# Fills on another engine, w1 kept in halves, masks in two ways and other orders of loads in an attention and expert kernel

## The chip, the cores and the metric

The kernel runs on one core of a Trainium2 chip. The time is device microseconds (us) of one execution; the kernel before took 395.87 us (median of 3 runs, 395.19 to 397.4). Five engines have queues of their own, each in order: TensorE (PE; its weight loads are listed as PEld), VectorE (DVE), ScalarE (ACT), GpSimd (POOL) and SyncE (SP, which only issues DMAs). Sixteen DMA engines move the data.

## The reference, cut to what matters

Attention over 4 batches, 8 heads, 768 positions and 64 numbers a head, and behind it a mixture of 4 experts that are all computed for every row:

```python
scores = q @ k.T / 8                       # causal
# heads 0, 2, 6 ("retrieval"): every earlier key
# heads 1, 3, 4, 5, 7 ("streaming"): keys 0..3 (sinks) and the last 64 keys
a = exp(scores - max); a = a / (a.sum() + 1e-9)
x = (a @ v) as rows of 8 * 64 = 512        # 3072 rows
p = domain_probs / (domain_probs.sum(-1) + 1e-9)
out = sum over e of p[:, e] * (relu(x @ w1[e]) @ w2[e])   # 512 -> 1024 -> 512
```

## The kernel before, in words

**Data.** w1 and w2 of all four experts are loaded once, cast to 16 bits by POOL's DMAs, and stay in SBUF (w1sb, w2sb). Rows are worked on in tiles of 128: four first tiles (the first 128 rows of each batch), then ten pairs of tiles. Attention goes in eight groups g = 2b + c (batch b, half c of 384 rows); the first tile of each batch is done by code of its own.

**The start (lines 381 to 482).** SP and ACT load q and k of the first tiles of batches 0 and 1 (load_first, L366), POOL everything else, in one written order: v of the first tiles, w1 of expert 0, q, k and v of the first tiles of batches 2 and 3, w2(0), w1(1), w2(1), w1(2), then k, q and v of group 0 (k_rows, q16, vR for the retrieval heads, vS for the windows of the streaming heads), w2(2) ahead of vS, the sinks (v_sinks, L285), w1(3), w2(3).

**Tiles 0 to 3 (L1497 to 1529).** For each: turn_first turns q and k on PE (L938), masks_first puts additive masks into PSUM by matmuls with the identity (L959), scores_first adds the scores to them (L971) and takes the exponential on ACT, values_first multiplies by v (L994), turn_back_first turns the result (L1015) into x_first. layer1_first (L1032) and plain_layer2 (L879) are expert 0.

**Experts 1 to 3 for the first tiles (moe_steps, L1465).** plain_steps: eight steps of layer 1 (L909, four matmuls of 512 columns each, Relu on ACT at L916), then layer 2 in two half steps for each of four tiles (L879, summed on DVE at L895). Between the steps small operations are put at numbered places: sums of weights (L795) for the Winograd form used later, prob_rows, and on ACT the fills (L1455): zeros in kS and kR, ones in vS, v_sinks and vR. A column of ones beside v makes the values matmul return the sum of the weights as well.

**The pairs (pair_steps, L1150).** Layer 1 plain (L1158) or in Winograd form (L1187), layer 2 in seven products of two halves (L1340). scale_inputs (L1109, DVE) scales xT, the attention's result, by the probabilities; before it, require(g) puts down whatever of group g is still missing.

**How attention is mixed in.** attention(b, c) (L489) is a generator that yields the estimated ns of each piece. The loop at the end (L1578) adds up the estimated time of the MoE steps and, by a plan of start and end for each group (L1545 to 1549), puts down attention steps until the group's own sum keeps pace. At a group's start it calls loads(a+1): k, q, and v of the retrieval heads of the next group (L209, L276). Within a group, in the order of heads 0, 2, 6, 1, 3, 5, 7, 4:

- turn_rows (group 0 only): k and q are turned on PE (L507). For all others SP does it by DMA transposes (transpose_rows, L229), put down in the group before: after the third head, or at the end of group 0.
- keys_to_rows (L244) and keys_to_windows in three parts (L262, L266, L270), DVE: copies of the turned keys for the retrieval and for the streaming heads.
- scores (L555, exponential L564, masks L571 and L575) and, some heads behind, values (L605 and L659).
- put_sinks (L295), a DMA that writes the sinks' rows into all windows of vS, issued by SP after the second head. The streaming heads' values (L659) read them.
- After a streaming head's values POOL loads the next group's window of v for that head (L278).
- The results go to xT: by SP transposes of x_one and x_pair (L641), and by DVE for the streaming heads (L679).

Of the kernel before, what the change touches and what calls it, by code (L numbers as in the profile page):

```python
# [19 lines left out]
def kernel(  # L20
# [34 lines left out]
    P = 128  # L55
# [46 lines left out]
    w1sb = pers.tile([P, E * DMP, F], FP16, name="w1sb")  # L102
# [27 lines left out]
    early = moe.tile([P, XS], FP16, name="early", tag="xs", bufs=1)  # L130
    warm = early[:, 1024:1536]
# [33 lines left out]
    def half(u):  # L165
        return slice(u * D, (u + 1) * D)
# [20 lines left out]
    def j0(c):  # L187
        return 0 if c else 1
# [40 lines left out]
    def transpose_rows(b, c):  # L229
        alloc_qT(b, c)  # L230
        for x, xr, at in ((kT, k_rows[b, c], P), (qTs[b, c], q16[b, c], 0)):
            for j in range(0 if at else j0(c), 3):
                nc.sync.dma_start(
                    out=x[:, :, at + j * P : at + (j + 1) * P],
                    in_=xr[:, j, :, :].rearrange("p h d -> p (h d)"),
                    transpose=True,
                )
# [54 lines left out]
    def put_sinks():  # L292
        x = windows(vSf).rearrange("p t s x -> p t (s x)")
        src = v_sinks.rearrange("p (t s) x -> p t (s x)", t=1)
        nc.sync.dma_start(out=x[0:NS, :, :], in_=src.to_broadcast([NS, WT, NSH * P]))  # L295

    def load_w1(e, f0, f1):
        x = moe_w1[e].rearrange("(u c d) f -> u d c f", u=2, c=DMP)
        for u in range(2):
            gp.dma_start(  # L300
                out=w1sb[half(u), e * DMP : (e + 1) * DMP, f0:f1],
                in_=x[u, :, :, f0:f1],
            )
# [5 lines left out]
    def w1_tile(e, ct, ft):  # L309

        return w_tile(e, w1sb[:, e * DMP + ct, :], ft)
# [54 lines left out]
    def load_first(eng, x, dst, b):  # L366
        x = x[b, :, 0:P, :].rearrange("(u h) (p j) d -> u p h (j d)", u=2, j=4)
        for u in range(2):
            eng.dma_start(out=dst[:, u, :], in_=x[u])
# [14 lines left out]
    for b in range(2):  # L384
        load_first(nc.sync, k, kf[b], b)
        load_first(nc.scalar, q, qf[b], b)
# [29 lines left out]
    fill(nc.vector, v_first[:, :, :, D : D + 2].rearrange("p b h x -> p (b h) x"), ONES)  # L416

# [3 lines left out]
    def warm_up(ps, n, cols):  # L421
# [5 lines left out]

    gp.memset(bias, 0.0)
    gp.affine_select(
        out=bias[:, 1, :], in_=bias[:, 1, :], compare_op=ALU.is_ge, fill=-60000.0,  # L430
        base=NW - 1, pattern=[[-1, P]], channel_multiplier=1,
    )
    gp.memset(bias[0:NS, 1, :], 0.0)
    gp.affine_select(
        out=bias, in_=bias, compare_op=ALU.is_ge, fill=-60000.0,
        base=0, pattern=[[0, 2], [1, P]], channel_multiplier=-1,
    )
# [18 lines left out]
    def load_first_all(b):  # L456
        for x, y, to in ((q, qf, qf_all), (k, kf, kf_all)):
            y[b] = to[:, b - 1, :, :].rearrange("p (u j) d -> p u (j d)", u=2)
            load_first(gp, x, y[b], b)
        load_first_v(b)  # L460

    load_first_v(1)
    load_w1(0, 0, F // 2)
    load_w1(0, F // 2, F)
    load_first_all(2)
    load_first_all(3)
    load_w2(0)
    load_w1(1, 0, F)
    load_w2(1)
    load_w1(2, 0, F)  # L470
# [7 lines left out]
    load_w1(3, 0, F)  # L478
# [10 lines left out]
    def attention(b, c):  # L489
# [218 lines left out]
        if g == 0:  # L708
            yield from turn_rows()
        keys_to_rows(b, c)  # L710
        yield 1500.0
        waiting = []
        for n, h in enumerate(order):
            v_steps, done = iter(()), None
            ahead = sum(len(score_tiles(x)) for x in (*waiting, h))
            if len(waiting) > 1 or (waiting and ahead > 6):
                done = waiting.pop(0)
                v_steps = values(done)
            for step in both(scores(h), v_steps):
                yield step  # L720
            if done is not None:
                behind_values(done)
            waiting.append(h)
            if n < 3:
                keys_to_windows(b, c, n)
                if c == 0:
                    yield 600.0
            if n == 1:
                put_sinks()
            if n == 2 and more and g:  # L730
                transpose_rows(*more)
# [3 lines left out]
        if g == 0:  # L735
            transpose_rows(*more)

    def small_things():
        def to_mask(x, bias):
            nc.vector.tensor_scalar(  # L740
                out=x, in0=bias, scalar1=0.0, scalar2=None, op0=ALU.is_ge
            )

        to_mask(mC, bias[:, 0, :])
        normalise(probs, psums, p_sb)

# [58 lines left out]
    def w1_part(e, j, k):  # L805
        c = e * DMP + j * KH
        return w1sb[:, c : c + KH, k * FN : (k + 1) * FN]
# [147 lines left out]
    def masks_first(b):  # L955
        ps_first[b] = [bank() for _ in range(2)]
        for u, ps in enumerate(ps_first[b]):
            for n in range(HG):
                nc.tensor.matmul(  # L959
                    out=ps[:, n * P : (n + 1) * P],  # L960
                    lhsT=ident16,
                    rhs=bias[:, 1 - RETR[u * HG + n], :].rearrange("m (p j) -> m j p", j=4),
                    start=(n == 0),
                    stop=False,
                    skip_group_check=True,
                )

    def scores_first(b):
        for n in range(HG):
            for u, ps in enumerate(ps_first[b]):  # L970
                nc.tensor.matmul(  # L971
                    out=ps[:, n * P : (n + 1) * P],
                    lhsT=qk_first[b][half(u), 1, n, :],
                    rhs=qk_first[b][half(u), 0, n, :],
                    start=False,
                    stop=True,
                    skip_group_check=True,
                )
        es_first[b] = []
        for ps in ps_first[b]:  # L980
            es = att.tile([P, 512], FP16, name="es", bufs=8)
            nc.scalar.activation(out=es, in_=ps, func=AF.Exp, scale=SC)
            es_first[b].append(es)
# [471 lines left out]
    def fills(i):  # L1455

        return [
            lambda: fill(nc.scalar, kSf[:, 0 : WT * NSH * P], 0.0),
            lambda: one_values(nc.scalar),
        ][2 * i :] + [  # L1460
            lambda: zero(nc.scalar, kR[i].rearrange("p c n t x -> p (c n) t x")),
            lambda: [one_values_r(nc.scalar, i, c) for c in range(NCH)],
        ]

    def moe_steps():  # L1465

        for e in range(1, E):
            sums = weight_sums(e - 1)
            sums.append(lambda e=e: last_weight_sum(e - 1))
            if e == E - 1:  # L1470
                more = first_weight_sums(EW[0])
                sums += more[:3]
            at = {}
            for n, op in enumerate(sums):
                at[n if e == E - 1 else 2 * n] = op
            if e == 1:
                at[FTP - 1] = prob_rows
                for n, op in enumerate(fills(0)):
                    at[FTP + 2 * n] = op
            if e == 2:  # L1480
                at[1] = lambda: load_probs(pair0)
                for n, op in enumerate(fills(1)):
                    at[FTP + 2 + 2 * n] = op
            if e == E - 1:
                at[FTP] = more[3]
                at[FTP + 1] = lambda: scale_inputs(pair0, 0)
                at[FTP + 3] = lambda: scale_inputs(pair0, EW[0])
                at[FTP + 5] = lambda: scaled_sums(EW[0])
            for n, step in enumerate(plain_steps(e)):
                yield step  # L1490
                if n in at:
                    at[n]()
        for n, nt0 in enumerate(pairs):
            yield from pair_steps(nt0, pairs[n + 1] if n + 1 < len(pairs) else None)


    nc.vector.memset(x_one[:, :, D:P], 0.0)  # L1497
    warm_up(ps_warm, 7, 512)
    masks_first(0)
    turn_first(0)  # L1500
    warm_up(pV.tile([P, 512], FP32, name="pV", bufs=2), 6, 128)
    scores_first(0)
    masks_first(1)
    values_first(0)
    turn_first(1)
    turn_back_first(0)
    scores_first(1)
    small_things()
    layer1_first(0, [0])
    values_first(1)  # L1510
    layer1_first(0, [1])
    turn_first(2)
    turn_back_first(1)
    masks_first(2)
    layer1_first(1, [0])
    scores_first(2)
    turn_first(3)
    masks_first(3)
    values_first(2)
    scores_first(3)  # L1520
    layer1_first(1, [1])
    turn_back_first(2)
    values_first(3)
    layer1_first(2)
# [22 lines left out]
    for a, n in zip(range(1, G), (0.75, 1.55, 2.55, 3.35, 4.35, 5.0, 6.65)):  # L1547
        plan[a] = (begin, first_pair + n * PAIR)
        begin = plan[a][1]
    state = {"a": 0, "steps": None, "done": 0.0}  # L1550

    def attention_step():

        a = state["a"]
        if state["steps"] is None:
            state["steps"] = attention(*divmod(a, NCH))
            state["done"] = 0.0
            if a < G - 1:
                loads(a + 1)
# [65 lines left out]
```

## Time and profile before

| | |
|---|---|
| median of 3 runs | 395.87 us (395.19 to 397.4) |
| profiled execution | 397.3 us, of which the trace spans 395.6 us |
| mean granted TensorE clock | 0.987 |
| busy: PE, PEld, DVE, ACT, POOL | 370.5, 310.4, 271.0, 227.6, 123.7 us |
| DMA | 40.41 MB, mean 102 GB/s; 62.8% of 16 engines' span in POOL's queue, 19.7% in that of SP and ACT |
| chain that ended last | PE 63%, DMA 12%, DVE 7%, POOL 7%, issue 5%, ACT 4% |
| first L1158 matmul (first pair of tiles) | at 93.67 us |

The busy rows tell how full an engine is over the whole span; the page's second part cuts the span into 40 slices of 9.89 us and shows the tenths of each slice that an engine was busy, the clock that the throttle granted PE, and the DMA engines' share. The list of waits says who waited for whom, with the sum, the number of times and the longest, all in us. In the time order of one engine each line has its start, its length, the line of code, the tile written and read, and in brackets the idle time before it with what ended it.

### The profile page before, as it was taken

What the parts mean: (1) busy time and instruction counts of PE and PEld (TensorE: products, weight loads), DVE (VectorE), ACT (ScalarE), POOL (GpSimd) and SP (SyncE); (2) the same over time, 40 slices, a digit from 0 to 9 for tenths busy, and PEclk for the clock granted to TensorE, in tenths of its full rate; (3) what the DMA queues carried; (4) which work ended last, traced back from release to release, by engine and by line L of the source; (5) the groups of instructions that cost most, each with busy time, mean ns of one, the idle gap of its engine ahead of it and who ended that gap; (6) DMA issues with size and microseconds to landing.
All of it is one profiled execution on the core that took longest, in us unless ns stands there. A gap on an engine that the chain in (4) does not pass through costs nothing.

```text
span 395.6 us, 10344 instructions
## 1 busy us (share of the span) xinstructions
PE 370.5 (94%) x4245; PEld 310.4 (78%) x4245; DVE 271.0 (68%) x599; ACT 227.6 (58%) x458; POOL 123.7 (31%) x160
## 2 busy tenths in 40 slices
PE   7799958998996899999999999899999999999997
PEld 4675423546985798899898899789899899998996
DVE  2544540789575768767967866966685976989882
ACT  2452517682865577778586696666477363351531
POOL 8672640746019308316637145610000000000000
PEclk9999996999999899999999999999999999999999
DMA  9999999999629969938999897991011030300101
GB/s 156 169 197 210 167 167 192 96 104 208 82 42 120 128 114 111 132 69 108 130 135 137 92 154 54 131 155 56 15 65 55 2 109 0 106 5 1 56 3 53
DMA packets 132744, 40.41 MB, mean 102 GB/s; under 512 B 119880, under 2 KB 125608, under 8 KB 132696
## 3 DMA queue, kind: packets, MB, share of 16 engines
q0 software_dynamic: 98400, 20.34, 62.8%
q1 hardware_dynamic: 33144, 17.84, 19.7%
q10 hardware_dynamic: 1152, 1.57, 1.3%
q8 instruction: 33, 0.54, 0.6%
q14 instruction: 15, 0.12, 0.1%
HBM read 47.00 MB, written 6.34 MB: 135 GB/s over the span
## 4 chain that ended last, share of the span: by engine, by line
PE 63%; DMA 12%; DVE 7%; POOL 7%; issue 5%; ACT 4%; SPq 0%; POOLq 0%; ACTq 0%; DVEq 0%
PE pO L1340 23%; PE pA L1158 18%; PE pO L1187 8%; DMA w1sb<-in_moe_w_dram 8%; PE pA L555 4%; DMA vS<-in_v_dram 2%; PE pA L909 2%; PE pV L1187 2%; POOL vS L278 2%; PE pA L1187 2%; PE pO L879 2%; PE pV L605 1%; DMA xT<-x_pair 1%; ACT rc L674 1%; PE pV L659 1%
## 5 line engine op out<-in xcount | busy, mean ns | idle before, releaser
L1340 PEld LDWEIGHTS <-hA 128*128 128x128 f16 x1104 | 104.9, 98 | 12.2
L1158 PE MATMUL pA<-xs,w1sb 128*128 128x256 f16 x768 | 98.0, 275 | 0.0
L1158 PEld LDWEIGHTS <-w1sb 128*128 128x128 f16 x768 | 72.5, 99 | 8.0
L1340 PE MATMUL pO<-w2sb,hA 128*128 128x256 f16 x640 | 78.0, 272 | 0.0
L1167 ACT ACTIVATE hA<-pA 128x512 f16<-128x512 f32 x96 | 56.5, 597 | 34.5 <-PE pA L1158 24.9
L564 ACT ACTIVATE es<-pA 128x384 f16<-128x384 f32 (+2 forms) x112 | 52.3, 493 | 28.4 <-PE pA L555 28.1
L278 POOL DMA_DIRECT2D vS<-in_v_dram x40 | 37.3, 936 | 97.7 <-PE pV L659 93.0
L1340 PE MATMUL pO<-tsb,hA 128*128 128x256 f16 x464 | 57.2, 273 | 0.0
L1109 DVE TENSOR_TENSOR xs<-xT,pB 128x512 f16<-128x512 f16 (+1 forms) x53 | 47.2, 914 | 4.4 <-DMA xT<-x_pair 3.0
L795 DVE TENSOR_TENSOR hA<-hA 128x1024 f16<-128x1024 f16 x60 | 39.5, 684 | 0.4
L1187 PEld LDWEIGHTS <-w1sb 128*128 128x128 f16 x512 | 31.3, 98 | 1.2 <-issue 0.4
L909 PE MATMUL pA<-x_first,w1sb 128*128 128x512 f16 x96 | 24.5, 408 | 6.7 <-ACT hA L916 6.7
L879 PE MATMUL pO<-w2sb,hA 128*128 128x512 f16 x128 | 29.7, 379 | 1.2 <-DVE acc L895 1.2
L679 DVE TENSOR_TENSOR xT<-pV,rc 64x256 f16<-64x256 f32 (+1 forms) x40 | 19.4, 488 | 11.3 <-ACT rc L683 10.5
L555 PE MATMUL pA<-qT,kR 128*128 128x128 f16 (+2 forms) x132 | 22.8, 266 | 3.4 <-DVE kR L244 3.4
L1360 ACT COPY s<-pO 128x256 f32<-128x256 f32 x31 | 11.5, 372 | 25.0 <-PE pO L1340 19.0
L209 POOL DMA_DIRECT2D k_rows<-in_k_dram x24 | 21.3, 896 | 14.2 <-PE pA L507 10.9
L1204 DVE CUSTOM_DVE_ANT_0 hA<-pO,s 128x512 f16<-128x512 f32 x26 | 17.7, 688 | 10.3 <-PE pO L1187 8.5
L1197 ACT COPY s<-pO 128x512 f32<-128x512 f32 x39 | 22.7, 588 | 3.2 <-PE pO L1187 2.9
L674 ACT ACTIVATE rc<-pV,eps 64x256 f32<-64x256 f32 (+1 forms) x40 | 20.9, 522 | 5.6 <-PE pV L659 4.5
L909 PEld LDWEIGHTS <-w1sb 128*128 128x128 f16 x96 | 9.5, 103 | 18.4 <-issue 9.8
L879 PEld LDWEIGHTS <-hA 128*128 128x128 f16 x128 | 12.2, 98 | 14.3 <-issue 1.7
(161 smaller groups left out, 542.0 us busy)
## 6 DMA issues: line engine op xcount, KB each, us to landing
pB<-p_rows SPq DMA_DIRECT2D x10, 512.0 KB, 4.1
out_dram<-o SPq DMA_DIRECT2D x19, 256.0 KB, 2.0
w2sb<-in_moe_w_dram POOLq DMA_DIRECT2D x4, 1024.0 KB, 12.3
w1sb<-in_moe_w_dram POOLq DMA_DIRECT2D x6, 512.0 KB, 11.9
k_rows<-in_k_dram POOLq DMA_DIRECT2D x24, 128.0 KB, 4.8
q<-in_q_dram POOLq DMA_DIRECT2D x20, 128.0 KB, 4.9
vS<-in_v_dram POOLq DMA_DIRECT2D x20, 112.0 KB, 4.5
vS<-in_v_dram POOLq DMA_DIRECT2D x20, 80.0 KB, 4.1
```

What stands on the lines that cost most here:

```text
L278: gp.dma_start(out=t[:, t0(c) :, own_v(h)], in_=windows_of(v, b, h, c))
L555: nc.tensor.matmul(out=ps[:, o : o + nq], lhsT=key_tile(b, c, h, t), rhs=qTs[b, c][:, hp, q0 : q0 + nq], start=True, stop=True,)
L564: nc.scalar.activation(out=es[:, 0:cols], in_=ps[:, 0:cols], func=AF.Exp, scale=SC)
L674: nc.scalar.activation(out=rc[r, lo:], in_=ps[o, lo:CH], func=AF.Ln, bias=eps[o, :])
L795: nc.vector.tensor_tensor(out=out, in0=a, in1=b, op=ALU.subtract)
L879: nc.tensor.matmul(out=ps_o, lhsT=hs[:, ft, nt * P : (nt + 1) * P], rhs=w2sb[:, e * FTP + ft, :], start=(ft == 0), stop=(ft == FTP - 1),)
L909: nc.tensor.matmul(out=ps, lhsT=w1_tile(e, ct, ft), rhs=x_first[:, ct, :], start=(ct == 0), stop=(ct == DMP - 1),)
L1109: nc.vector.tensor_tensor(out=o, in0=xin, in1=pb.to_broadcast([P, DMP, n, P]), op=ALU.mult)
L1158: nc.tensor.matmul(out=ps[:, f * PC : (f + 1) * PC], lhsT=w1_tile(e, ct, f0 + f), rhs=xs[:, ct, :], start=(ct == 0), stop=(ct == DMP - 1),)
L1167: nc.scalar.activation(out=blocks[:, b0 : b0 + 2, k0 : k0 + 2, :].rearrange("p t f x -> p f t x"), in_=ps.rearrange("p (f t x) -> p f t x" ...
L1187: nc.tensor.matmul(out=ps[:, f * P : (f + 1) * P], lhsT=w_tile(e, w[:, ct, :], f), rhs=a[:, ct, :], start=(first and f == 0 and ct == 0), ...
L1340: nc.tensor.matmul(out=ps, lhsT=a[:, k, :], rhs=b(k), start=(first and k == 0), stop=(k == KT - 1), skip_group_check=not first,)
```

## The change

1. The ones in vS, v_sinks and vR are filled by DVE at the very start instead of by ACT in experts 1 and 2. ACT keeps the zeros.
2. w1sb is laid out by expert and half of the 1024 columns, and loaded half by half: four DMAs an expert instead of two (expert 0 had four before).
3. Tiles 0 and 1 get their additive masks ahead of everything else on PE, with the bias laid out so that the matmuls read it in order; tiles 2 and 3 have no mask matmuls, but a multiplication by 0 and 1 on DVE after the exponential. Six short warm-up matmuls go. The order of the first tiles' steps is another one.
4. q and k of batches 0 and 1 are spread differently over SP and ACT; w1's halves lie between the first rows of batches 2 and 3.
5. The next group's loads are put down two groups ahead (loads(g+2) after the sixth head); group 1's, after turn_rows of group 0.
6. The transposes of q for the next group come at a group's start, those of k after its first head; in group 0 both after the fourth head.
7. keys_to_windows: part 0 at the start, parts 1 and 2 after the first head, with one 600 ns step instead of three.
8. put_sinks is issued by POOL, at a group's start, instead of by SP after the second head.
9. Sums of weights, scale_inputs and the plan's ends are moved.

```diff
-    w1sb = pers.tile([P, E * DMP, F], FP16, name="w1sb")
+    w1sb = pers.tile([P, E * 2, DMP, F // 2], FP16, name="w1sb")
...
-        nc.sync.dma_start(out=x[0:NS, :, :], in_=src.to_broadcast([NS, WT, NSH * P]))
+        gp.dma_start(out=x[0:NS, :, :], in_=src.to_broadcast([NS, WT, NSH * P]))
...
-    for b in range(2):
-        load_first(nc.sync, k, kf[b], b)
-        load_first(nc.scalar, q, qf[b], b)
+    for eng, x, y, b, u in (
+        (nc.scalar, q, qf, 0, 0), (nc.scalar, q, qf, 0, 1), (nc.scalar, k, kf, 0, 1),
+        (nc.sync, k, kf, 0, 0), (nc.sync, k, kf, 1, 0), (nc.sync, k, kf, 1, 1),
+        (nc.scalar, q, qf, 1, 0), (nc.sync, q, qf, 1, 1),
+    ):
+        load_first(eng, x, y[b], b, u)
...
+    one_values(nc.vector)
+    for i in range(2):
+        for c in range(NCH):
+            one_values_r(nc.vector, i, c)
...
     load_first_v(1)
-    load_w1(0, 0, F // 2)
-    load_w1(0, F // 2, F)
-    load_first_all(2)
-    load_first_all(3)
+    load_w1(0, 0)
+    load_first_rows(2)
+    load_w1(0, 1)
+    load_first_rows(3)
+    load_first_v(2)
+    load_first_v(3)
     load_w2(0)
...
         if g == 0:
             yield from turn_rows()
+            loads(1)
+        elif more:
+            transpose_q(*more)
+        put_sinks()
         keys_to_rows(b, c)
+        keys_to_windows(b, c, 0)
         yield 1500.0
...
-            if n < 3:
-                keys_to_windows(b, c, n)
+            if n == 0:
+                keys_to_windows(b, c, 1)
+                keys_to_windows(b, c, 2)
+                if more and g:
+                    transpose_k(*more)
                 if c == 0:
                     yield 600.0
-            if n == 1:
-                put_sinks()
-            if n == 2 and more and g:
-                transpose_rows(*more)
+            if n == 3 and not g:
+                transpose_k(*more)
+                transpose_q(*more)
+            if n == 5 and g + 2 < G:
+                loads(g + 2)
         for h in waiting:
             yield from values(h)
             behind_values(h)
-        if g == 0:
-            transpose_rows(*more)
...
+    def masks_behind():
...
+            nc.vector.tensor_scalar(
+                out=out, in0=src.to_broadcast(list(out.shape)), scalar1=0.0,
+                scalar2=None, op0=ALU.is_ge,
+            )
...
             nc.scalar.activation(out=es, in_=ps, func=AF.Exp, scale=SC)
+            if not masked:
+                nc.vector.tensor_tensor(
+                    out=es, in0=es,
+                    in1=mask_first[:, u, :, :].rearrange("p h x -> p (h x)"),
+                    op=ALU.mult,
+                )
...
+            lambda: zero(nc.scalar, kR[i].rearrange("p c n t x -> p (c n) t x")),
             lambda: fill(nc.scalar, kSf[:, 0 : WT * NSH * P], 0.0),
...
+        put(E - 1, 5, lambda: scale_inputs(pair0, 0))
+        put(E - 1, FTP, more[3])
+        put(E - 1, FTP + 2, lambda: scale_inputs(pair0, EW[0]))
+        put(E - 1, FTP + 4, lambda: scaled_sums(EW[0]))
...
+    masks_behind()
     warm_up(ps_warm, 7, 512)
     masks_first(0)
+    masks_first(1)
     turn_first(0)
-    warm_up(pV.tile([P, 512], FP32, name="pV", bufs=2), 6, 128)
     scores_first(0)
-    masks_first(1)
+    turn_first(1)
     values_first(0)
-    turn_first(1)
-    turn_back_first(0)
     scores_first(1)
...
-    for a, n in zip(range(1, G), (0.75, 1.55, 2.55, 3.35, 4.35, 5.0, 6.65)):
+    for a, n in zip(range(1, G), (0.7, 1.55, 2.55, 3.4, 4.4, 5.3, 6.65)):
...
-            if a < G - 1:
-                loads(a + 1)
```

## The prediction

> **What bounds the kernel now.** I read the page's busy shares and slices first, then the waits, then the chain and the stretches where PE idles.
>
> ```profile
> PE 370.5 (94%) x4245; PEld 310.4 (78%) x4245; DVE 271.0 (68%) x599; ACT 227.6 (58%) x458; POOL 123.7 (31%) x160
> ...
> PE   7799958998996899999999999899999999999997
> ...
> PEclk9999996999999899999999999999999999999999
> DMA  9999999999629969938999897991011030300101
> ```
>
> PE works in 370.5 of 395.6 us, so only its 25 us of idle time and its slow stretches can be won. The dips in PE's row are slice 5, slice 12 and a shallow one near slice 25; the first two come with a lower clock. The DMA row is full for the first ten slices: until about 99 us nothing lands earlier just because it is asked for earlier. The waits and the two-microsecond stretches (PE, PEld, DVE, ACT, POOL busy, clock, DMA share, GB/s) name hole 1:
>
> ```profile
> ACT vS L343 <- DMA vS<-in_v_dram: 11.1, 1, 11.1
> ```
> ```profile
> 54.00:56.00 2.00, 0.49 (x3) 0.10 (x1) 0.48 (x1) 0.00 (x0) 0.59 (x2) 1.00 2.27 149
> 56.00:58.00 2.00, 0.00 (x0) 0.00 (x0) 0.00 (x0) 0.08 (x1) 2.00 (x3) 1.00 0.72 47
> 58.00:60.00 2.00, 0.00 (x0) 0.00 (x0) 0.00 (x0) 2.00 (x5) 0.13 (x1) 0.79 0.95 170
> 60.00:62.00 2.00, 0.76 (x2) 0.26 (x2) 0.00 (x0) 2.00 (x6) 0.00 (x0) 0.50 1.09 195
> 62.00:64.00 2.00, 2.00 (x6) 0.76 (x5) 0.00 (x0) 1.22 (x3) 0.00 (x0) 0.50 1.10 186
> ```
>
> ACT's fill of ones in vS waits 11.07 us for the window loads of v, which land at 57.8; the Relus behind it wait too; PE runs out of banks and idles 6.75 us (54.49 to 61.24). Then the granted clock is 0.50 until about 66, so 4.8 us of matmuls do 2.4 us of work. Hole 1 is 9.2 us. Hole 2, in time order on DVE:
>
> ```profile
> 124.70 0.56 DVE L679 TENSOR_TENSOR xT<-pV,rc 64x384 f16<-64x384 f32 x1
> 128.28 1.22 DVE L1109 TENSOR_TENSOR xs<-xT,pB 128x1024 f16<-128x1024 f16 x1 [3.01 <-DMA xT<-x_pair]
> 129.42 0.83 DVE L244 COPY kR<-kT 64x768 f16<-64x768 f16 x2
> ```
>
> x_pair was ready at 117.34, but SP issued its transpose at 122.75, after five transposes of k and q (3.83 + 3.62 us). PE idles 3.37 us (126.45 to 129.82), then runs at half clock from 131 to 134: 3.4 + 1.7 = 5.1 us. Hole 3 (251 to 258.6, attention group 6, clock 1.00) is 2.7 us: v rows landing late, then values waiting for DVE.
>
> **Which transfers wait on POOL.** One pattern decides my forecast:
>
> ```profile
> 27.29 0.88 POOL L209 DMA_DIRECT2D k_rows<-in_k_dram  x1 [1.19 <-DMA w2sb<-in_moe_w_dram]
> ...
> 37.69 0.76 POOL L276 DMA_DIRECT2D vR<-in_v_dram  x1 [4.50 <-DMA w2sb<-in_moe_w_dram]
> ...
> 55.41 0.54 POOL L285 DMA_DIRECT2D v_sinks<-in_v_dram  x1 [4.67 <-DMA w2sb<-in_moe_w_dram]
> ```
>
> Counting POOL's DMAs in order, these are the 25th, 28th and 39th, and each waits for the one eight before it (17th, 20th, 31st, all w2): POOL has eight in flight. They also land in order: the first vS load, issued at 45.25 behind w2 of expert 2, lands 10.4 us later.
>
> **The change part by part.** All sums are against the profiled execution, 397.3 us (span 395.6 plus 1.7 around it); the median of the runs shown is 395.87, 1.4 lower.
>
> *Ones on DVE.* ACT loses 1.21 + 0.41 + 0.30 + 0.31 us of copies and the wait. DVE gains two fills of 448 and 672 words; from its 256-word fill (L402, 0.27 us) 0.5 and 0.7, with the small ones 1.6 us. They lie in DVE's idle 2.66 to 8.41, while PE waits for q and k, as do the three mask fills (0.9 us by L740's 0.18 for 128 columns, after POOL's bias at 4.0). Nothing on the path; if that cover went, 2.5 us.
>
> *Masks.* Sixteen L959 matmuls of tiles 2 and 3 go: 2 x 1.09 us on a dense PE. Four DVE multiplies come, 0.45 us each by L571's 0.36 for 384 columns, with layer-1 matmuls emitted in between. The other masks move into the wait for q (5.93).
>
> *First loads.* The second half of k of batch 0 becomes ACT's third DMA instead of SP's second: 0 to +1 us at 7.28; I take +0.6, one issue.
>
> *w1 in halves.* The wait at 14.28 (1.40 us) goes. POOL issues 16 instead of 10 w1 DMAs, 6 x 0.64 = 3.8 us, hidden in its waits of 4.50 and 4.67; the bytes are the same. w2 of expert 0 still lands at 27.05, and its layer 2, now at 28.37, can start 1.3 us earlier at most. So expert 1 starts 1.5 us earlier (0 to 3).
>
> *Hole 1's place.* Without it PE would reach the streaming heads' values of group 0 far earlier. Following the loop at the end of the file by hand: two of the three 600 ns steps go, so more of group 0 is put down per MoE step, and head 1's values move from expert 3's second tile to the end of expert 2. Expert 2 starts at 50.87 - 1.5; then 7.07 + 7.07 us of L909 and L879, 1.2 of turns and 4.9 of scores and values as their rows last: head 1's values are reached at about 70.5, latencies included.
>
> They read vS with the sinks in it. put_sinks leaves SP (59.47 before) for POOL, behind the nine DMAs of loads(1). By the count of eight, loads(1)'s second vR waits for w2 of expert 3, and put_sinks, the 58th, for the second k load. w2 of expert 3 lands at 70.4 (57.19 + 13.2). The same kinds of loads of group 0 moved 784 KB from 42.6 to 47.6, so the 912 KB of loads(1) take 5.8 us and the sinks land at 70.4 + 5.8 + 0.3 = **76.5**. PE idles 6 us there. This wait takes hole 1's place. Bounds: 73 (as soon as POOL can issue) to 80.
>
> The Trainium skill, DMA: Bandwidth & Descriptors, section "Queues, rings and completion order", says that a DMA engine alternates between queue rows packet by packet and consumes one row's ring in order; so the same 35 KB from SP's row would not stand behind k, q and vR. The trace's 10.4 us of the vS load agrees for POOL's row. By that rule the sinks left on SP would land near 60, and the sum would be that of rival A below.
>
> After 76.5 PE has seven score and value blocks (2.0 us), expert 3's 32 + 32 matmuls (6.9 + 6.9) and the half clock (2.2, between holes 1 and 2): the first pair starts at 76.5 + 18.0 = 94.5, against 93.67. **+0.8.** The move of weight sums and of scale_inputs to step 5 adds no instruction; x_pair, now behind six transposes of 1.25 us on SP, lands near 81, before DVE asks (about 85): hidden.
>
> *Holes 2 and 3.* Loads two groups ahead, q turned at a group's start and k after its first head leave SP free when x_pair is ready: -5.1 (bounds -2 to -5.1: DVE is busy 6.6 of the 9 us from 126, and the window copies now come together). Hole 3: rows of v are long there, and group 6 is spread from 5.3 pairs on: -2.7 (0 to -2.7). Of PE's small waits at 116 to 123 (1.55 us) half: -0.8.
>
> *put_sinks in later groups.* Its chain from a group's first streaming values: vS and sinks issues 0.9 + 1.8, loads 7.7, four vS 3.6, landing 4.5, put_sinks 3.2: 21.5 us. By the new order the next group's first streaming values come 20 us later in group 2 and 18.7 in group 4, by a count of dense matmuls that ignores DVE. 0 to 4.3 us; I take +1.5, a third, since DVE (above 0.9 busy around 186 to 198) paces PE there.
>
> **Sum.** +0.8 - 5.1 - 2.7 - 0.8 + 1.5 = -6.3 us: 391.0 for the profiled execution, 389.6 at the median; I say 389.5.
>
> **Rivals.**
> - *A: the sinks land in time*, before PE asks. For it: hole 1's cause does vanish. Against: the count of eight. Then x_pair behind q's transposes (q lands 75.5; x_pair 81) holds DVE at scale_inputs; PE has banks for two tiles of layer 2 and starts the pair near 88.5: -5.2 - 7.1, **383.5**.
> - *B: nothing takes hole 1's place*: -9.2 - 1.5 - 7.1, **378**. It needs k, q and v of group 1 some 8 us earlier, and the DMA row is full.
> - *C: holes 2 and 3 fill again* because DVE, not SP, bounds those stretches (252 to 262: DVE 0.9 and more): only 2 of 8.6 us come, **396**.
> - *D, slower: put_sinks on POOL is late in groups 2 and 4.* If DMA contention adds 4 us to its landing (the vS loads at 45 took 10 instead of 4.5), the stalls are 5.5 and 6.8 us, each with 2 us of half clock: 16.3 instead of 1.5, **404**. It decides from where these stalls exceed 1.5 + 6.3 = 7.8 us together.
> - That the fills don't do what they say has no room: nothing writes vS before the fills on DVE.
>
> **Chances.** Forecast 0.52, A 0.17, B 0.07, C 0.12, D 0.12. The forecast's own range is 386 to 393. With A and C in and B and D out (0.19), 382 to 397. A measurement of this kernel tells 0.5% (2 us) from no change: faster is the forecast, A and B and a little of C, 0.78; same most of C, 0.10; slower D, 0.12.
>
> **What would show it.** No ACT wait at the fill of ones. PE idle at head 1's values of group 0, waiting for vS, and clock 0.50 after it (A and B: none, or DVE waiting for x_pair instead). First L1158 near 94.5. x_pair's transposes issued within 2 us of their x_pair, PE dense where hole 2 was. The forecast is wrong if the sinks of group 0 land well before or after 76.5, or if PE waits for vS in groups 2 and 4.

## The result and the profile after

The changed kernel takes 407.34 us (median of 4 runs, 404.0 to 409.3) against 395.53 (4 runs, 394.99 to 397.4): a ratio of 1.028, 95% interval 1.020 to 1.036. The forecast was 389.5, with 397 as the upper end: wrong in sign. Ratios here leave out executions that were disturbed, so that a ratio need not be the quotient of the medians beside it.

The profiled execution took 404.0 us (span 402.3, mean clock 0.975), 6.7 more than the one of before. It is the shortest of its four, and the one of before the longest of its; the other 5 us of the medians' difference lie in executions without a trace. From the page, busy rows and slices (10.06 us each):

```profile
PE 368.9 (92%) x4223; PEld 309.2 (77%) x4223; DVE 273.0 (68%) x614; ACT 224.8 (56%) x450; POOL 132.3 (33%) x175
...
PE   7779997099997989999499999999999999999997
...
PEclk9999999579998999999989999999999999999999
```

PE's row has no dip in slice 5 any more (hole 1 is gone, and no wait of ACT for vS is left), but slice 7 is empty, slices 7 and 8 have a clock of 0.5 and 0.7, and slice 19 is a new dip. The waits, and in time order of PE the four lines that hold most of its idle time behind 69 us:

```profile
PE pV L678 <- DMA vS<-v_sinks: 17.5, 3, 11.6
```
```profile
80.78 0.39 PE L678 MATMUL pV<-es,vS 128*128 128x32 f16 x5 [11.55 <-DMA vS<-v_sinks]
...
125.05 0.34 PE L678 MATMUL pV<-es,vS 128*128 128x48 f16 x7 [2.27 <-DVE xT L698]
...
142.07 0.29 PE L678 MATMUL pV<-es,vS 128*128 128x32 f16 x5 [1.37 <-DMA vS<-v_sinks]
...
201.80 0.37 PE L678 MATMUL pV<-es,vS 128*128 128x32 f16 x5 [4.61 <-DMA vS<-v_sinks]
```

Three times PE stands at a group's first streaming values and waits for the sinks in vS: 11.55 us in group 0, 1.37 in group 2, 4.61 in group 4. The clock falls with them: in stretches (columns PE, PEld, DVE, ACT, POOL, clock, DMA share, GB/s) it is already 0.50 while PE still waits:

```profile
70.00:72.00 2.00, 0.00 (x0) 0.00 (x0) 1.04 (x3) 0.00 (x0) 0.66 (x1) 0.87 2.35 157
74.00:76.00 2.00, 0.00 (x0) 0.00 (x0) 0.00 (x0) 0.00 (x0) 0.38 (x1) 0.50 2.39 155
78.00:80.00 2.00, 0.00 (x0) 0.00 (x0) 0.00 (x0) 0.00 (x0) 0.00 (x0) 0.50 1.68 113
```

What POOL issued in that time:

```profile
71.34 0.77 POOL L283 DMA_DIRECT2D vR<-in_v_dram  x1 [4.63 <-DMA w2sb<-in_moe_w_dram]
72.30 0.77 POOL L283 DMA_DIRECT2D vR<-in_v_dram  x1 [0.18 <-issue]
73.70 0.68 POOL L302 DMA_DIRECT2D vS<-v_sinks  x1 [0.63 <-issue]
```

put_sinks is the last of ten DMAs of group 0's start. The second vR load waits for w2 of expert 3, as the count of eight had it; the sinks are issued at 73.70 and land 7.0 us later. The first pair of tiles starts at 97.63 instead of 93.67 (+4.0), and from there to the end the kernel takes 304.7 us instead of 301.9 (+2.7).

### The profile page after: what moved, and what is told of

Its sections match the earlier page's. It is cut to its first block, busy times and chain, and to the rows that moved or that the text cites. A ratio compares the mean times of both kernels' runs of the same rounds, so it can differ in the third digit from the quotient of the medians.

```text
span 402.3 us, 10304 instructions
## 1 busy us (share of the span) xinstructions
PE 368.9 (92%) x4223; PEld 309.2 (77%) x4223; DVE 273.0 (68%) x614; ACT 224.8 (56%) x450; POOL 132.3 (33%) x175
## 4 chain that ended last, share of the span: by engine, by line
PE 45%; DVE 3%; DMA 1%; ACT 1%; issue 0%; DVEq 0%
PE pO L1389 18%; PE pA L1207 12%; PE pO L1236 7%; PE pA L574 2%; PE pV L1236 2%; PE pA L1236 1%; DMA vS<-v_sinks 1%; PE pV L678 1%; DVE hA L836 1%; PE pV L624 1%; DVE xs L1158 1%; DVE xT L698 1%; PE pA L1481 0%; ACT hA L1216 0%; DVE o L1412 0%
## 5 line engine op out<-in xcount | busy, mean ns | idle before, releaser
L1389 PEld LDWEIGHTS <-hA 128*128 128x128 f16 x1104 | 106.5, 99 | 14.0 <-DVE hA L836 0.6
L1207 PE MATMUL pA<-xs,w1sb 128*128 128x256 f16 x768 | 97.0, 273 | 0.0
L1207 PEld LDWEIGHTS <-w1sb 128*128 128x128 f16 x768 | 71.7, 98 | 7.4
L583 ACT ACTIVATE es<-pA 128x384 f16<-128x384 f32 (+2 forms) x112 | 51.4, 495 | 26.6 <-PE pA L574 23.8
L594 DVE TENSOR_TENSOR es<-es,mW 128x256 f16<-128x256 f16 (+1 forms) x40 | 12.7, 321 | 32.5 <-ACT es L583 32.4
L1236 PEld LDWEIGHTS <-w1sb 128*128 128x128 f16 x512 | 31.2, 98 | 1.5 <-issue 0.7
L678 PE MATMUL pV<-es,vS 128*128 128x56 f16 (+2 forms) x240 | 13.1, 189 | 20.2 <-DMA vS<-v_sinks 17.5
L698 DVE TENSOR_TENSOR xT<-pV,rc 64x256 f16<-64x256 f32 (+1 forms) x40 | 19.5, 489 | 14.7 <-ACT rc L702 14.0
L678 PEld LDWEIGHTS <-vS 128*128 128x128 f16 x240 | 11.4, 98 | 22.2 <-DMA vS<-v_sinks 12.0
L949 PE MATMUL pA<-x_first,w1sb 128*128 128x512 f16 x96 | 23.5, 400 | 0.0
L919 PEld LDWEIGHTS <-hA 128*128 128x128 f16 x128 | 12.1, 98 | 13.4 <-ACT hA L956 0.3
```

The lines of the kernel that those rows point to most:

```text
L583: nc.scalar.activation(out=es[:, 0:cols], in_=ps[:, 0:cols], func=AF.Exp, scale=SC)
L678: nc.tensor.matmul(out=ps[:, q0 : q0 + nq], lhsT=v_tiles(b, c, h)[:, t, :], rhs=es[:, o : o + nq], start=(n == 0), stop=(n == len(work) - ...
L698: nc.vector.tensor_tensor(out=xT[g][r, ct, lo:], in0=ps[r, lo:CH], in1=rc[r, lo:], op=ALU.mult)
L919: nc.tensor.matmul(out=ps_o, lhsT=hs[:, ft, nt * P : (nt + 1) * P], rhs=w2sb[:, e * FTP + ft, :], start=(ft == 0), stop=(ft == FTP - 1),)
L949: nc.tensor.matmul(out=ps, lhsT=w1_tile(e, ct, ft), rhs=x_first[:, ct, :], start=(ct == 0), stop=(ct == DMP - 1),)
L1207: nc.tensor.matmul(out=ps[:, f * PC : (f + 1) * PC], lhsT=w1_tile(e, ct, f0 + f), rhs=xs[:, ct, :], start=(ct == 0), stop=(ct == DMP - 1),)
```

## The experiments

The theory, T1: put_sinks in POOL's queue, behind loads(1), costs the time. The rivals: other parts of the change cost it (T2), or the place in POOL's queue has no effect and only the late issue counts (T1b). Each kernel ran beside the kernel before on the same chip.

**1. The ones alone.** Before, with the fills of ones moved to VectorE's start:

```diff
+    one_values(nc.vector)
+    for i in range(2):
+        for c in range(NCH):
+            one_values_r(nc.vector, i, c)
...
-            lambda: one_values(nc.scalar),
...
-            lambda: [one_values_r(nc.scalar, i, c) for c in range(NCH)],
```

> The kernel before with one part of the change: the fills of ones in vS, v_sinks and vR are done by VectorE at the start; the zeros stay with ScalarE, put_sinks with SyncE. T1 (the loss of the changed kernel comes from put_sinks standing behind POOL's loads): with the sinks left on SP, nothing takes hole 1's place but the loads themselves: ScalarE's 11.1 us wait for vS goes, PE is dense at 54 to 61, the first pair of tiles starts near 85 to 88 instead of 93.67, total 387 to 390 (6 to 9 us less than before's 395.5). T2 (hole 1 is only the face of a limit by the transfers, which would show at the next place, w1 and w2 of expert 3 landing near 63 and 70): the first pair starts at 91 to 94, total 393 to 396.

386.99 us (385.95 to 388.01) against 396.31; ratio 0.978 (0.973 to 0.982). The first pair starts at 85.66, 8.0 earlier. Its page:

```profile
PE   8799999989987999999999999799999999999996
...
PEclk9899999999999999999999999999999999999999
```

Hole 1 is gone and the clock holds from slice 2 on. This part of the change gives the upper end of T1's 6 to 9 us, as long as SP puts the sinks.

**2 and 3. put_sinks on POOL alone, and with the ones.** In both one line is changed, at the old place behind the second head; the second of the two has the ones of experiment 1 as well:

```diff
-        nc.sync.dma_start(out=x[0:NS, :, :], in_=src.to_broadcast([NS, WT, NSH * P]))
+        gp.dma_start(out=x[0:NS, :, :], in_=src.to_broadcast([NS, WT, NSH * P]))
```

> The kernel before with one part of the change: put_sinks is issued by POOL at its old place, after the second head. T1: in group 0 it stands behind loads(1) in POOL's queue and lands near 80, and the streaming heads' values of group 0 are asked for near 79 there (ScalarE's wait for vS has already delayed everything by 9 us), so only 0 to 2 us are lost there; in later groups the sinks land some 3 us later than from SP: total 396 to 399. T2 (put_sinks on POOL costs nothing, the other parts of the change do): 395 to 396. If the queue hurts in groups 2 and 4 by itself: 400 or more, with PE waits for vS of 4 us and more there.

403.45 us (398.78 to 405.41); ratio 1.015 (1.008 to 1.022). More than T1's 396 to 399. In the profiled execution, the longest of the four, hole 1 is still there (PE idles 8.81 us, 6.75 before), and PE waits 1.75 us for the sinks in group 0, 1.11 in group 4 and 4.07 in group 6.

> The kernel before with both: ones by VectorE at the start and put_sinks issued by POOL at its old place, after the second head. T1: the gain of the first is eaten by the second: PE reaches the streaming heads' values of group 0 near 70 and waits until the sinks land near 78 to 81, half clock after it; the first pair of tiles starts at 94 to 98, total 396 to 402, and the difference to the kernel with the ones alone is 8 us or more. T2 (put_sinks on POOL costs nothing): as the kernel with the ones alone, within 2 us.

407.13 us (404.92 to 408.38); ratio 1.028 (1.023 to 1.032): the changed kernel's time, from two of its nine parts. Against experiment 1 one line costs 20.1 us. In time order on PE and POOL:

```profile
80.02 0.39 PE L663 MATMUL pV<-es,vS 128*128 128x32 f16 x5 [9.67 <-DMA vS<-v_sinks]
...
259.35 0.37 PE L663 MATMUL pV<-es,vS 128*128 128x32 f16 x5 [4.32 <-DMA vS<-v_sinks]
```
```profile
70.98 0.78 POOL L276 DMA_DIRECT2D vR<-in_v_dram  x1 [4.22 <-DMA w2sb<-in_moe_w_dram]
...
73.35 0.68 POOL L295 DMA_DIRECT2D vS<-v_sinks  x1 [0.64 <-DVE tsb L799]
```

The same wait at the same place as in the changed kernel; the first pair starts at 96.23, 10.6 us behind experiment 1. The other 9 us come behind that, in later groups: PE idles 3.9 us more there and loses 5.4 us to the clock, which experiment 1 does not lose. Half of that follows the 4.32 us wait in group 6, the other half hole 2, where PE waits 4.07 us for kR instead of 2.31. T2 is out for group 0.

**4. The changed kernel with put_sinks on SP, at its new place.**

```diff
-        gp.dma_start(out=x[0:NS, :, :], in_=src.to_broadcast([NS, WT, NSH * P]))
+        nc.sync.dma_start(out=x[0:NS, :, :], in_=src.to_broadcast([NS, WT, NSH * P]))
```

> The changed kernel with one part undone: put_sinks is issued by SyncE again, at the new place (a group's start). T1: PE's 11.6 us wait for vS in group 0 goes, as the sinks land near 60 to 62; the first pair of tiles starts at 88 to 91 instead of 97.6 (x_pair behind six transposes on SP may then hold VectorE); the waits in groups 2 and 4 get shorter by the 3 us that the landing took in POOL's queue: total 394 to 397 against 407.3. T2 (the masks, the window copies, the order of loads cost the time): first pair 96 or later, total 404 to 407.

395.06 us (10 runs, 392.2 to 399.66); ratio 0.996 (0.992 to 0.999). The sinks are issued at 57.41, no engine waits for them in group 0, and the first pair starts at 87.84: 9.8 us earlier than in the changed kernel. In the medians this line is worth 12.3 us, all of the change's loss, as T1 said. On SP and PE:

```profile
57.41 0.82 SPq L302 DMA_DIRECT2D vS<-v_sinks  x1
```
```profile
69.52 0.29 PE L678 MATMUL pV<-es,vS 128*128 128x32 f16 x5 [0.15 <-DVE es L594]
```

But three waits stay:

```profile
84.32 3.68 PE L919 MATMUL pO<-w2sb,hA 128*128 128x512 f16 x16 [2.51 <-DVE acc L935]
...
131.56 0.29 PE L678 MATMUL pV<-es,vS 128*128 128x32 f16 x5 [1.49 <-DMA vS<-v_sinks]
...
190.50 0.37 PE L678 MATMUL pV<-es,vS 128*128 128x32 f16 x5 [3.82 <-DMA vS<-v_sinks]
```

The first is rival A's: VectorE waits 2.67 us for x_pair, whose transpose stands on SP behind six others. The other two show that the engine of put_sinks is not what makes it late in groups 2 and 4 of this order of work.

**5. put_sinks on POOL, but ahead of loads(1).**

```diff
         if g == 0:
             yield from turn_rows()
+            put_sinks()
             loads(1)
```

> The changed kernel with one step moved: in group 0 put_sinks goes ahead of loads(1), still in POOL's queue. In later groups nothing changes. T1a (POOL's DMAs land in the order in which they were issued): the sinks are issued near 59, but land behind w1 and w2 of expert 3, near 70.5 to 71.5; PE, which asks at 69, waits 1.5 to 2.5 us instead of 11.6, with little half clock: total 393 to 396 against 407.3. T1b (what cost the time is only the late issue, behind the nine loads; landing takes 3 to 4 us from any queue): the sinks land near 63, PE doesn't wait for them at all in group 0: the same total less 2 to 4 us. T2 (PE's wait has another cause than the place in POOL's queue): 404 or more. The waits in groups 2 and 4 (1.4 and 4.6 us) stay in all cases.

397.5 us (10 runs, 394.14 to 402.53); ratio 1.000 (0.996 to 1.004). On POOL and PE:

```profile
58.92 0.94 POOL L333 DMA_DIRECT2D w2sb<-in_moe_w_dram  x1
59.83 0.66 POOL L302 DMA_DIRECT2D vS<-v_sinks  x1
```
```profile
72.16 0.40 PE L678 MATMUL pV<-es,vS 128*128 128x32 f16 x5 [3.39 <-DMA vS<-v_sinks]
```

Issued at 59.83, the 35 KB land 12.3 us later, just behind w2 of expert 3. The earlier issue is worth 9.8 us, but T1b, which had the sinks land near 63, falls: on POOL they do not pass what is already in its queue. The Trainium skill (DMA: Bandwidth & Descriptors, section "Queues, rings and completion order") says that each DMA engine consumes one row's ring in order; these 12.3 us agree.

From SP they do pass it. In experiment 1 SP issued the sinks at 59.91, behind w2 of expert 3 (57.46 on POOL, landed at 69.6), and the view of the DMA queues has their 32 packets between 64 and 66. In experiment 4 it has them between 61.5 and 63.5, 4 to 6 us after the issue, while POOL's queue moved 0.33 MB; w2 landed at 69.5. So "nothing lands earlier just because it is asked for earlier", which the prediction read from the full DMA row, held within POOL's queue, not between SP's and POOL's.

**6, 7 and 8. What keeps the sinks late in groups 2 and 4.** My theory P was POOL's order: loads(g+2) ahead of vS's loads. From experiment 4, one step at a time:

```diff
-            if n == 5 and g + 2 < G:
-                loads(g + 2)
...
             behind_values(h)
+        if g + 2 < G:
+            loads(g + 2)
```

> The changed kernel with put_sinks on SyncE and one more part undone: loads(g+2) stand at the end of a group, behind the next group's four or five loads of vS, instead of after the sixth head. Theory P: the waits for vS that are left with put_sinks on SyncE (1.49 us in group 2, 3.82 in group 4, with 2 to 4 us of lower clock) come from vS's loads standing behind the eight of loads(g+2) on POOL (7.7 us of issuing): they go, 395.1 becomes 387 to 390. Rival Q (vS is loaded late because its values are computed late, not because of POOL's order): the waits stay within 1 us, 394 to 396. Rival R: the loads that were moved back are now late (k, q, or v rows at the next group's start), 392 to 396 with waits for kT or vR in place of vS.

414.72 us (414.14 to 415.69); ratio 1.046 (1.042 to 1.050): 20 us worse, which no theory foresaw. VectorE now waits 9.80 us for x_pair in group 0, PE behind it 9.64, and the waits for vS in groups 2 and 4 stay (2.42 and 3.93 us). In group 6 PE stands 5.91 us before the same values; there the trace names no releaser.

```profile
81.71 1.21 SPq L660 DMA_TRANSPOSE xT<-x_pair  x1
```
```profile
88.76 1.23 DVE L1158 TENSOR_TENSOR xs<-xT,pB 128x1024 f16<-128x1024 f16 x1 [9.80 <-DMA xT<-x_pair]
```

x_pair's transpose is issued at 81.71 and takes until 88.76; in experiment 4 it was issued at 79.18 and VectorE went on at 81.66. With loads(2) out of the way POOL issues five loads of vS up to 79.35, of which four came at 86.95 and later in experiment 4, and the DMA share from 80 to 82 is 2.13 instead of 0.54. The next step puts group 0's transposes behind it:

```diff
-            if n == 3 and not g:
-                transpose_k(*more)
-                transpose_q(*more)
...
+        if not g:
+            transpose_k(*more)
+            transpose_q(*more)
         if g + 2 < G:
```

> As the kernel with put_sinks on SyncE and the loads at the end of a group, and also: in group 0 the six transposes for group 1 stand on SyncE at the end, behind x_pair's, as in the kernel before. If x_pair behind them is what holds VectorE 2.7 us and PE 2.5 us at 82 to 84: the first pair of tiles starts at 85.3 to 86 instead of 87.8, total 1.5 to 2.5 us under the kernel without this step. If those transposes are then late for group 1 (k and q turned near 77 to 82, needed when group 1 starts): no gain or a loss of up to 2 us.

404.75 us (402.05 to 406.23); ratio 1.019 (1.012 to 1.025). It takes 10 us off: x_pair's place was the 9.64 us. The waits in groups 2, 4 and 6 are 3.75, 3.97 and 5.80 us. On SP, in group 2:

```profile
124.10 4.67 SPq L231 DMA_TRANSPOSE qT<-q  x3
129.01 0.68 SPq L302 DMA_DIRECT2D vS<-v_sinks  x1
```

vS's loads had been issued by 116.75, yet put_sinks stands behind three transposes, and these wait for q, which POOL issues only from 119.38 to 121.98. POOL's order was not it; SP's is. So put_sinks goes ahead of them:

```diff
-        elif more:
-            transpose_q(*more)
         put_sinks()
+        if more and g:
+            transpose_q(*more)
```

> The kernel with put_sinks on SyncE, the loads at a group's end and group 0's transposes last (404.75 us), and one more step: put_sinks stands ahead of the transposes of q on SyncE instead of behind them. Theory S (in groups 2, 4 and 6 put_sinks stands on SyncE behind three transposes of q, which wait for q rows that POOL has only just been asked for): the PE waits for vS in groups 2, 4 and 6 (3.75, 3.97 and 5.8 us, each with lower clock behind it, some 18 us together) go, total 386 to 390. Rival (the sinks are late because vS's own loads are): the waits stay over 2 us each, 398 or more. If q is then late instead: waits for qT at the groups' starts, 390 to 398.

388.46 us (387.69 to 389.0) against 397.4; ratio 0.978 (0.974 to 0.981). PE waits nowhere for vS; theory S holds, with 16.3 us from one step.

**9. The loads back at the change's place.** From experiment 8:

```diff
+            if n == 5 and g + 2 < G:
+                loads(g + 2)
...
-        if g + 2 < G:
-            loads(g + 2)
```

> The mended kernel (put_sinks on SyncE ahead of q's transposes, group 0's transposes last; 388.46 us) with one step put back as in the change: loads(g+2) after the sixth head, ahead of most of the next group's vS loads on POOL. If the order on POOL matters by itself: PE waits for vS in groups 2 and 4 return at 1.5 and 3.8 us, with lower clock after the second, and the total is 393 to 397. If only put_sinks behind q's transposes mattered: no such waits, 387 to 390.

384.99 us (383.97 to 385.51) against 396.73; ratio 0.971 (0.964 to 0.979), the lowest median of all. P was wrong once more: with put_sinks first, loads two groups ahead do no harm that can be measured. No wait for vS is left in group 2 and one of 1.37 us in group 4. The same place in experiment 4 and here, on POOL and SP, shows why:

```profile
178.35 3.50 POOL L285 DMA_DIRECT2D vS<-in_v_dram  x4
```
```profile
177.70 4.17 SPq L231 DMA_TRANSPOSE qT<-q  x3
186.88 0.69 SPq L302 DMA_DIRECT2D vS<-v_sinks  x1
```
```profile
174.92 3.50 POOL L285 DMA_DIRECT2D vS<-in_v_dram  x4
```
```profile
180.83 0.68 SPq L302 DMA_DIRECT2D vS<-v_sinks  x1
181.56 4.50 SPq L231 DMA_TRANSPOSE qT<-q  x3
```

In experiment 4 SP has finished the transposes at 181.9, but put_sinks goes out at 186.88, 5.0 us after the last vS load was issued; here it is 2.4 us. Both times the issue must wait for the vS loads to land, and beside three transposes they land 2.6 us later. The view of the DMA queues shows both at once: from 180 to 186 in experiment 4 POOL's queue moved 0.35 MB and SP's 0.34, from 175 to 181 here POOL's moved 0.49 and SP's nothing.

**10. Why the sinks landed at 80.8 and not at 76.5.** The changed kernel, with group 0's transposes held back on SP until head 1's values are there:

```diff
-            if n == 3 and not g:
-                transpose_k(*more)
-                transpose_q(*more)
...
+        if not g:
+            ct, u = PLACE[SH[0]]
+            nc.sync.dma_start(out=gate[half(u), :], in_=xT[g][half(u), ct, P : P + 16])
+            transpose_k(*more)
+            transpose_q(*more)
```

> The changed kernel (put_sinks on POOL behind loads(1)), but group 0's six transposes for group 1 are held back on SyncE until the result of head 1's values is there, by a copy of 2 KB put ahead of them; x_pair's now goes ahead of them. Nothing else changes. The question is why the sinks landed at 80.8 and not at 76.5, as loads(1) at group 0's rate would have it. Theory V (the six transposes, issued from 72 to 80.7, share the DMA engines with the last loads and the sinks): the sinks land at 76.5 to 78, PE's wait falls from 11.6 to 7 to 9 us, total 402 to 405 if the transposes are early enough for group 1. Rival W (loads(1) and the 35 KB of sinks take that long by themselves): the sinks land at 80 to 81 as before, total 406 to 410. In both cases the transposes come 8 us later; if group 1 waits for them, PE idles near 100 and the total tells nothing: the landing does.

405.27 us (402.35 to 406.73); ratio 1.022 (1.018 to 1.026). PE waits 7.99 us and goes on at 78.41. Measured from the end of POOL's wait for w2, the sinks come after 8.2 us (70.23 to 78.4) instead of 9.4 (71.34 to 80.8). So by this one pair of executions the transposes cost about 1.2 us; the rest is elsewhere, as these stretches show:

```profile
74.00:75.00 1.00, 0.00 (x0) 0.00 (x0) 0.00 (x0) 0.00 (x0) 0.00 (x0) 0.50 1.86 107
75.00:76.00 1.00, 0.00 (x0) 0.00 (x0) 0.00 (x0) 0.00 (x0) 0.00 (x0) 0.50 0.86 66
76.00:77.00 1.00, 0.00 (x0) 0.00 (x0) 0.00 (x0) 0.00 (x0) 0.00 (x0) 0.50 0.20 26
77.00:78.00 1.00, 0.00 (x0) 0.00 (x0) 0.00 (x0) 0.00 (x0) 0.00 (x0) 0.50 0.00 0
```

The rate (last column) falls from 107 GB/s to 66 and 26 as the last transfers end; after 77.0 nothing moves, and PE still waits 1.4 us. The Trainium skill (DMA: Bandwidth & Descriptors, section "Anatomy of one DMA — SWDGE (gpsimd) path") puts the fixed cost of a DMA at about 2 us and most of that after the last byte; 1.4 us here is of that kind. 78.4 lies between what V and W expected: V holds in part.

**11 and 12. The kernel before, taken further.** From experiment 1, the transposes of q go behind the sixth head:

```diff
             if n == 2 and more and g:
-                transpose_rows(*more)
+                transpose_rows(*more, (0,))
+            if n == 5 and more and g:
+                transpose_rows(*more, (1,))
```

> The kernel before with ones by VectorE, and one step for hole 2: the transposes of q for the next group stand on SyncE after the sixth head instead of after the third, so that x_pair's no longer stands behind them; those of k stay. If x_pair behind five transposes is the cause of hole 2 (PE idle 2.3 us at 118 to 121 with the ones alone): x_pair's transpose is issued near 111 instead of 114.4, that idle time falls under 1 us, total 385 to 386 against 387.0. If VectorE is the limit there: PE waits as long for its copies, 386.5 to 387.5. If q is then late: over 388.

386.0 us (384.6 to 386.74) against 396.83; ratio 0.973 (0.969 to 0.978). x_pair's transpose is issued at 111.89 instead of 114.44, and PE's idle time of hole 2 falls from 2.31 to 0.61 us, so SP's order caused most of hole 2; against 386.99 the ranges overlap. So do they with experiment 9: the changed kernel, mended, is not measurably faster than this one with two small steps. Then the first half of w1 ahead of v of batch 1's first tile:

```diff
-    load_first_v(1)
     load_w1(0, 0, F // 2)
+    load_first_v(1)
```

> The kernel before with ones by VectorE and q's transposes after the sixth head (386.0 us), and one more step: the first half of w1 of expert 0 is asked for ahead of v of batch 1's first tile. If the transfer of that half is what PE waits for at 14.7 to 17 (2.26 us): it lands up to 1.5 us earlier, the wait shrinks to under 1 us, and the total is 384.5 to 385.5, less if w2 of expert 0 then becomes what expert 0 waits for near 28. If v of batch 1 is then late: a wait for it of about 1 us, 386 to 387.

386.51 us (385.21 to 387.62); ratio 0.976 (0.970 to 0.982). PE's wait for w1 falls from 2.26 to 1.45 us, not under 1, and no gain can be measured. The trace has waits that experiment 11 does not have: 2.24 us for xs where hole 2 was, 1.03 for the sinks.

## Why the prediction was wrong, step by step

On the profiled executions it gave -6.3 us and +6.7 came.

- **Hole 1's place, "+0.8": the place was right, the size failed.** The wait at head 1's values of group 0, its cause and the lower clock came as written. PE arrived at 69.2 instead of 70.5. But "the sinks land at 70.4 + 5.8 + 0.3 = 76.5" failed: they landed at 80.7, past the upper bound of 80. The rate behind the 5.8 us, 157 GB/s, held: from 71.3 to 76 all queues together moved 155. Left out were w2's later end (71.3), the end of the burst, and the release. From 76 to 79 the transposes on SP moved 0.36 MB and POOL's queue only 0.12; its last packet was through at 78.8, and the release came 1.9 us behind it. PE waited 11.55 us instead of 6, and 16.85 us of work behind it (18.0 forecast) make 97.63: +4.0.
- **The front, 1.5 us earlier (0 to 3): 0.4.** w1's wait went, but expert 1 starts at 36.70 instead of 37.06. PE waits elsewhere instead: 1.08, 0.69 and 0.64 us at L1064, for VectorE's division of the values by their sums (L1056; 0.21 us in all at this place before), and for x_first. The new order of the first tiles leaves less work between values_first and turn_back_first, and the forecast had no term for that. The multiplications by the masks (L1027) were covered as forecast; PE waits for none of them itself.
- **Hole 2, "-5.1": -1.1.** x_pair is no longer late, but 8 us before the old place PE waits 2.27 us for VectorE's scaling of xT (L698) and loses 1.7 us to the clock, 4.0 instead of 5.1. The bound of -2 was not low enough. This is the mechanism of rival C, VectorE instead of SP. The 1.7 us are chance in part: most kernels with this wait do not lose them (last section).
- **Hole 3, "-2.7": -2.2.** 0.46 us of idle time from 252 to 264 are left. The small waits, "-0.8": all 1.55 us went.
- **put_sinks late in later groups, "+1.5": +7.4**, that is 1.37 + 4.61 us of waiting and 1.4 of clock in group 4. The chain of 21.5 us was near: it took 22.3 us in group 2 and 23.1 in group 4, and PE was there after 21.0 and 18.5 (20 and 18.7 forecast). The step that failed is the third: I had the wait at 0 to 4.3, took 1.5 of it because VectorE would hold PE back, and no clock. The cause that I gave, POOL's queue, was wrong too: experiment 4 keeps the waits with SP, experiments 8 and 9 remove nearly all of them by SP's order. I had looked at q's transposes only as a gain for hole 2; moved to a group's start, they run beside vS's loads, and the chain had no term for that; in experiment 9 it takes 19.9 us in group 4.
- **Rivals.** D named 404, close to what came, but for stalls in groups 2 and 4 that are 6.0 us and not the 12.3 it needed; group 0 gave the rest: near by luck. A's pair at 88.5, with VectorE held by x_pair, is experiment 4's 87.84. A's sum, 383.5, is near experiment 9 (385.0) by luck: there x_pair is not late, the pair starts at 85.94, and behind it 4.1 us are won where A had 7.1.

The sum of the rows: +4.0 at the first pair, then -1.1 - 2.2 - 1.55 + 7.4 = +2.6, against 2.7 measured. Of the 13.0 us between forecast and result 5.9 lie in the later groups, 4.0 in hole 2 and 3.2 in group 0's sinks.

What stays open: the 5 us by which the other executions of the changed kernel exceed the profiled one, and in experiments 2 and 3 why hole 2's wait grows and what of group 6's is the queue's.

## What to carry to other kernels

A small DMA that a matmul soon needs belongs in a queue with little in it: in POOL's, 35 KB landed 7 to 12 us after the issue, behind whatever stood there; from SP its packets were through 6 us after the issue with the same bulk under way. This one line cost 12 us in the changed kernel and 20 in experiment 3. When a wait is removed, look up what the engine reaches next and when that lands, and count the landing as issue, bytes at the rate that the other queues leave, and the time after the last byte (1.4 and 1.9 us here). Put the DMA that is needed first ahead of those that only prepare the next group, on the issuing engine's list as well as among the transfers: here that one step was worth 16 us, and the changed kernel mended so is 2.9% faster than the one before.

## What the runs showed of the hardware that was not expected

The same idle time cost the clock once and not another time. The wait for L698 is 2.27 us in the changed kernel and in experiment 8, with the same instructions around it. The stretches of the first and then of the second:

```profile
124.00:126.00 2.00, 0.95 (x15) 0.90 (x16) 1.97 (x4) 1.14 (x3) 2.00 (x4) 1.00 1.38 88
126.00:128.00 2.00, 2.00 (x18) 1.50 (x16) 0.65 (x2) 1.89 (x4) 2.00 (x3) 0.52 2.11 141
```
```profile
112.00:114.00 2.00, 0.96 (x15) 0.91 (x16) 1.97 (x4) 1.14 (x3) 0.51 (x2) 1.00 1.32 90
114.00:116.00 2.00, 2.00 (x26) 1.77 (x24) 0.65 (x2) 1.89 (x4) 1.76 (x3) 1.00 0.62 39
```

PE is as busy in both, but the clock is 0.52 in one and 1.00 in the other, and 18 matmuls against 26 get done in 2 us. Eight kernels have this wait of 2.27 us; the clock falls behind it in two, the changed kernel and experiment 7's, and stays at 1.00 in six. The Trainium skill (TensorE: Matmul & The Clock Gate, "Part 1: The HAM clock gate") has the clock follow PE's activity in windows of 3.4 us that run freely. If part of a window is enough, its phase would decide; no run here shows where a window begins. Its advice to avoid gaps of more than about 3 us was not enough here: 2.27 us cost 1.7 us more. Which short wait is punished so, no view of the trace foretells.

And a transpose of x_pair that takes 2.5 us from issue to use in experiment 4 takes 7.0 in experiment 6, with five loads of vS just ahead of it: in those 7 us POOL's queue moved 0.65 MB beside SP's 0.46, in the 2.5 us of experiment 4 SP's moved alone. The 1.2 us of experiment 10 and the 2.6 us between experiments 4 and 9 point the same way: transposes and loads slow one another.
